# A fused attention and two-layer kernel: the value products of a turned head pair are placed behind the first run of scores, with a PSUM bank from another ring

## The chip, the cores and the metric

The kernel runs on one core of a Trainium2 chip. The metric is the device time of one execution in microseconds. Three runs of the kernel before gave 1013.64, 1014.48 and 1014.77 us; the median, 1014.48 us, is the number to be predicted for the changed kernel.

## What is computed

```python
scores = q @ k.T / 8                       # 8 batches x 8 heads, 576 x 576, head size 64
decay = cum[:, :, :, None] - cum[:, :, None, :]   # cum: running sum of log f
attn = softmax(where(causal, -1e9, scores + decay))
x = (attn @ v), heads side by side          # 4608 rows x 512
h = x @ w_in                                # 512 -> 2048
g = max(h, 0) + alpha * min(h, 0)
out = g @ w_out                             # 2048 -> 512
```

The matrix products are taken in parts (a high and a low half of each operand, three products for one), so that the result has more digits than one pass gives.

## The kernel before

**Work.** Heads go in 32 pairs (`n`, four pairs to a batch). Two heads of a pair share TensorE: each takes one half of it. Pairs 0 to 8 transpose their exponentials on TensorE; pairs 9 to 31 are *turned* (`turned`, L806): VectorE transposes blocks of 32x32 and sixteen DMAs put the blocks where they belong. When the four pairs of a batch are done, that batch of the first layer (`ffn1`: 16 groups of twelve 128x512 products, each group in one PSUM bank) can run. The second layer follows the attention.

**A turned pair on TensorE.** There are three pieces, all issued through `mm` (L364), so that the trace tells them by their tiles:

- *run 1* (L859 to L866, 24 matmuls, `bank<-Qhl`, 64 rows of the array by 128 columns): the scores of four query tiles, t3, t2, t0 and t1, of both heads. It takes six PSUM banks: `bA`, `bB`, `bC`, two each.
- *run 2* (L891 to L897, 6 matmuls, `bank<-Qhl`, the whole 128x128 array): the scores of the 64 tail queries of both heads. It writes one bank of its own, `bD`, and the free upper half of `bC[0]`, of which t1 of the first head fills the lower half.
- *the values* (`values` and `pv`, L933 to L953, 60 matmuls in the trace, `bank<-big,vr`, 128 rows by 64 columns): the exponentials of the pair **two before**, times v. The list `behind` holds the pairs whose values wait; `turned(n)` takes the oldest when there are two (L900). They write `bX` and 64 free columns of `bC[1]`, whose first 256 hold t1 of the second head. `done` then copies both with ScalarE (L958, L959).

The values need the sixteen moves of that pair (L919, half issued by SyncE, half by GpSimd, 100 KB each, `big<-big`), and its v (`vr`). This happens for n = 11 to 31, 21 times; the last two pairs' values have banks of their own at the end of pair 31 (L966).

**VectorE for a turned pair.** `shrink` (L846) adds the decay to a tile of scores and takes its minimum, reading PSUM: t3, t2, t0, then t1. `turn` (L879) transposes, in three parts; the tail's two reductions are L909. ScalarE takes the exponentials (L826).

**Order.** All operations are first listed with a cost, a due key, their dependencies and the ring that each buffer comes from. `Plan.run` (L116) then goes through time: on each engine it takes the operation that can start first, of equal starts the one with the lowest key. It does this before anything is issued; each engine's instructions then stand in that order. Costs are spread by a seeded random factor of up to 3% that is drawn as the operations are listed. The first layer has a key near 1e6 and so fills whatever TensorE has left; its evacuation has the key -1000 and goes first.

**Rings.** The eight PSUM banks are one store with rings on it: `rP` (turned pairs; at most 6), `rV` (values; at most 2; used by pair 8 alone), `rH` (first layer; 2 to 4), and others. A ring with `least` keeps that many banks from the others while it holds fewer; `rH.least` is 2 from the start and 0 once the last batch of the first layer is through. `swap_banks` (L1090) sets `rP.least` to 4 when the turned pairs begin.

```python
ns = 250 + c_row(512, 3) + c_row(384, 3) + c_row(128, 3) + c_row(256, 3)
s1 = s = op("PE", ns, run1, k0, rdy, bA + bB + bC + held)
...
bD, bX = Buf(rP), Buf(rP)
...
s = op("PE", ns, run2, k0 + 5, rdy, bC + [bD, bX] + held)
...
if len(behind) > 1:
    fn, vd, vb, done = behind.pop(0)(bX, bC[1])
    done(op("PE", ns_v, fn, k0 + 5.01, [s] + vd, [bX, bC[1]] + vb))
```

Of the kernel before, what the change touches and what calls it, by code (L numbers as in the profile page):

```python
# [94 lines left out]
class Plan:  # L95
# [7 lines left out]
    def op(self, eng, ns, fn, key, deps=(), bufs=(), two=False, kb=0.0):  # L103
        o = Op()
        ns *= self.rnd.uniform(0.97, 1.03)
        o.eng, o.ns, o.fn, o.key, o.bufs, o.two, o.kb = eng, ns / 1000.0 * SLACK.get(eng, 1.0), fn, key, bufs, two, kb
        o.outs, o.ready, o.end, o.n = [], 0.0, None, 0
        for b in bufs:
            b.left += 1
        for d in deps:  # L110
            if d is not None and d.end is None:
                d.outs.append(o)
                o.n += 1
            elif d is not None:
                o.ready = max(o.ready, d.end + self.lag(d, o))
        self.ops.append(o)  # L116
        return o
# [88 lines left out]
def attention_moe(  # L206
# [18 lines left out]
    op = plan.op  # L225
# [28 lines left out]
    rH, rO = Ring(banks, 2, 4), Ring(banks, 0, 6)  # L254
    rP, rV, rC = Ring(banks, 0, 6), Ring(banks, 0, 2), Ring(banks, 0, 1)
# [53 lines left out]
    def c_mm(n):  # L309
        return max(110, 13.3 + 0.4175 * n)  # L310

    def c_m4(n):
        return 5 + 1.67 * n

    def c_row(n, m):
        return m * max(110, 13.3 + 0.4175 * n)
# [226 lines left out]
    behind, later_x, quick_ops, value_ops, last_e = [], [], [], [], []  # L543
# [262 lines left out]
    def turned(n):  # L806

        b, p = divmod(n, NP)
        k0 = NS * n
        kl = k0 - 16  # L810
        held = []
        rdy, rz, rt, bZ, terms = load_n(n, held)
# [25 lines left out]
        def shrink(i, h, src, st, s, bank):  # L838
            w, col = 128 * (i + 1), (i if h == 0 else 5 + i)
            bE, e = block(i, h)  # L840

            def red():
                blk = lambda ap: ap.rearrange("p (j s) -> p j s", s=128)
                z = blk(bZ.t[0][:, h])
                in1 = (z[:, 6:7], z[:, 0:8:7], z[:, 0:9:4], z[:, 0:4])[i]
                ve.tensor_tensor_reduce(out=blk(e()), in0=blk(src()), in1=in1, scale=-0.125,  # L846
                                        scalar=3.0e38, op0=ALU.add, op1=ALU.min, accum_out=lo()[:, col : col + 1])

            r_ = op("DVE", c_dve(w) + 80, red, st, [s] + rz[h], [bank, bE, bst, bZ])
            expo(bE, e, w, col, st, [r_])  # L850
# [5 lines left out]
        bC = [Buf(rP), Buf(rP)]  # L856
# [7 lines left out]

        ns = 250 + c_row(512, 3) + c_row(384, 3) + c_row(128, 3) + c_row(256, 3)
        s1 = s = op("PE", ns, run1, k0, rdy, bA + bB + bC + held)  # L866
        for i, t, bank in ((3, t3, bA), (2, t2, bB), (0, t0, bB)):
            for h in range(2):
                shrink(i, h, lambda t=t, h=h: t(h), k0 + 0.1 * (4 - i), s, bank[h])
# [15 lines left out]
        turn(bE1, TA, CUT, k0 + 3, sums[3:], TA)  # L885
        seen = len(sums)

        bD, bX = Buf(rP), Buf(rP)
        part = ((0, 320, lambda: bD.t[:, 0:320]), (320, S, lambda: bC[0].t[:, 256:512]))

        def run2():  # L891
# [2 lines left out]
                    mm(out(), q()[:, 512:640], k()[:, c0:c1], c == 0, c == 2)  # L894

        ns = 100 + 6 * c_mm(288)
        s = op("PE", ns, run2, k0 + 5, rdy, bC + [bD, bX] + held)  # L897
        for h in (1, 0):
            shrink(1, h, lambda h=h: t1(h), k0 + 3.5, s1, bC[h])
        if len(behind) > 1:  # L900
            fn, vd, vb, done = behind.pop(0)(bX, bC[1])
            done(op("PE", ns_v, fn, k0 + 5.01, [s] + vd, [bX, bC[1]] + vb))

        e5 = lambda: bE2.t[:, 128 * (TAIL - CUT) : 128 * (TAIL - CUT) + S]

# [60 lines left out]
        while n == B * NP - 1 and behind:  # L966
            own = [Buf(rP) for _ in range(2)]
            fn, vd, vb, done = behind.pop(0)(*own)
# [34 lines left out]
    ns_v = 10 * c_m4(128) + 5 * c_m4(64) + 250  # L1003
# [80 lines left out]
    def swap(*what):  # L1084
        for st, ts in what:
            st.items += ts
            st.free += [(plan.t, i) for i in range(len(ts))]
        rT.least = 0

    def swap_banks():  # L1090
        swap((rE.store, [e_1]), (rE2.store, [e_2]))
        rS.least = 0
        rP.least = 4

    o_swap = op("-", 0, swap_banks, 0, last_e)
    op("-", 0, lambda: swap((rTa.store, [0, 1]), (rTb.store, [t_t])), 0, w_all + last_e)
    op("-", 0, lambda: swap((rM.store, m_t)), 0, [value_ops[-1]])
    op("POOL", 100, lambda: po.memset(e_0[:, 128 * TAIL + S :], 0.0), NS * NX - 22, [o_swap])
    for n in range(NX, B * NP):
        turned(n)  # L1100
# [298 lines left out]
```

## Time and profile before

| | us |
|---|---|
| runs | 1013.64, 1014.48, 1014.77 (median 1014.48) |
| span of the profiled execution | 1010.1 |
| TensorE busy in the span | 1004.1 (99%) |
| VectorE, ScalarE, GpSimd busy | 801.8, 614.0, 385.0 |

The profile's own execution is told by its span, first to last instruction; no time of its own stands beside it. The median of the runs is 4.4 us above that span. In the rows, PE is TensorE, DVE VectorE, ACT ScalarE, POOL GpSimd, SP SyncE; L364 is line 364 of the kernel. A timeline row gives start, length, engine, line, operation, output and input tiles, shape and the number of instructions merged in it. Matmuls are pipelined, so the ends of rows overlap the next row's start by some tenths of a us: the time that a block of matmuls takes is read from its start to the start of the next block.

### The profile page before, as it was taken

The page shows a single profiled execution, that of the slowest core. Times are in us where ns is not written, and L with a number is a line of the kernel's source. Part 1 is how long each engine was busy: PE and PEld are TensorE (multiplying, and loading weights), DVE is VectorE, ACT ScalarE, POOL GpSimd, SP SyncE. Part 2 cuts the span into 40 slices and gives each one's busy share as a digit, 9 for nine tenths or more (in the row PEclk, how much of TensorE's full clock was granted, in tenths as well). Part 3 has the DMA queues.
Part 4 walks back from the last instruction along what each step waited for, and adds up shares of the span by engine and source line. Part 5 has one row for each costly group of instructions (what it writes and reads, how often), then busy time and mean ns, then how long its engine had stood idle before and what let it go on. Part 6 is the DMA issues. An engine that isn't in the chain of part 4 may idle for free.

```text
span 1010.1 us, 22277 instructions
## 1 busy us (share of the span) xinstructions
PE 1004.1 (99%) x7928; PEld 894.0 (88%) x7928; DVE 801.8 (79%) x1745; ACT 614.0 (61%) x1379; POOL 385.0 (38%) x625
## 2 busy tenths in 40 slices
PE   9999999999999999999999999999999999999998
PEld 6788888888888888888888888999999999999998
DVE  6887778778778838777646888688898888989994
ACT  7888886666666646666444766564554645546551
POOL 4554658899898848877640100000000000000000
PEclk9999999999999999999999999999999999999999
DMA  6977856988888876878766665633434344434411
GB/s 206 263 228 235 263 142 187 279 260 253 255 242 248 239 219 202 243 222 254 209 194 231 210 231 185 209 111 120 152 123 143 111 144 131 140 112 139 136 53 43
DMA packets 130687, 191.14 MB, mean 189 GB/s; under 512 B 22088, under 2 KB 79728, under 8 KB 130576
## 3 DMA queue, kind: packets, MB, share of 16 engines
q1 hardware_dynamic: 124400, 170.66, 54.5%
q0 software_dynamic: 5888, 18.85, 6.9%
q8 instruction: 63, 1.03, 0.4%
q14 instruction: 48, 0.39, 0.1%
q10 hardware_dynamic: 288, 0.20, 0.1%
HBM read 102.74 MB, written 48.80 MB: 150 GB/s over the span
## 4 chain that ended last, share of the span: by engine, by line
PE 96%; DMA 2%; DVE 1%; issue 0%; DVEq 0%; ACT 0%; SPq 0%
PE bank L364 92%; PE bank L584 3%; DMA big<-big 1%; PE bank L466 1%; DVE big L879 1%; DMA hd<-hs 0%; PE bank L432 0%; DMA xt<-xs 0%; DVE hs L1036 0%; DVE big L846 0%; PE bank L651 0%; PE bank L725 0%; DVE hs L1327 0%; DVE big L429 0%; ACT hs L1034 0%
## 5 line engine op out<-in xcount | busy, mean ns | idle before, releaser
L364 PE MATMUL bank<-xx,wi 128*128 128x512 f32 x1728 | 412.3, 394 | 0.0
L364 PEld LDWEIGHTS bank<-xx,wi 128*128 128x128 f32 x1728 | 318.7, 188 | 69.0 <-DVE st L846 0.3
L826 ACT ACTIVATE big<-big,st 128x384 f32<-128x384 f32 (+4 forms) x207 | 119.2, 578 | 56.3 <-DVE st L846 53.0
L364 PE MATMUL bank<-wi,gh 128*128 128x256 f32 x1008 | 123.9, 283 | 0.0
L364 PE MATMUL bank<-wot,gh 128*128 128x256 f32 x1008 | 123.9, 283 | 0.0
L364 PEld LDWEIGHTS bank<-wot,gh 128*128 128x128 f32 x1008 | 122.3, 192 | 0.1
L364 PEld LDWEIGHTS bank<-wi,gh 128*128 128x128 f32 x1008 | 122.3, 192 | 0.0
L1034 ACT ACTIVATE hs<-bank,ab 128x512 f32<-128x512 f32 x96 | 65.6, 684 | 86.4 <-PE bank L364 58.0
L879 DVE STREAM_TRANSPOSE big<-big 128x1408 f32<-128x1408 f32 (+2 forms) x69 | 87.1, 1275 | 24.6 <-DMA hd<-hs 10.5
L1036 DVE SCALAR_TENSOR_TENSOR hs<-bank,sa,hs 128x512 f32<-128x512 f32 x96 | 70.3, 734 | 45.2 <-ACT hs L1034 44.5
L538 POOL TENSOR_TENSOR Qhl<-rqk,Qhl 128x640 fp32r<-128x640 f32 (+1 forms) x56 | 83.4, 1500 | 54.9 <-ACT Qhl L537 43.6
L919 POOL DMA_DIRECT2D big<-big x184 | 92.0, 507 | 14.7 <-issue 8.8
L364 PE MATMUL bank<-big,vr 128*64 128x128 f32 (+2 forms) x1884 | 95.5, 259 | 0.4 <-DVE st L609 0.2
L364 PEld LDWEIGHTS bank<-big,vr 128*64 128x64 f32 x1884 | 88.9, 137 | 7.6 <-DVE st L703 0.8
L364 PE MATMUL bank<-Qhl 64*128 64x512 f32 (+6 forms) x840 | 90.8, 323 | 0.7 <-DVE hs L1036 0.7
L364 PEld LDWEIGHTS bank<-Qhl 64*128 64x128 f32 (+1 forms) x840 | 76.6, 186 | 16.5 <-issue 6.3
L510 POOL TENSOR_TENSOR Z<-Z,tri 128x384 f32<-128x384 f32 x60 | 54.8, 923 | 32.8 <-DMA Z<-c 17.3
L846 DVE CUSTOM_DVE_ANT_1 big<-bank,Z 128x384 f32<-128x384 f32 (+1 forms) x92 | 41.8, 483 | 30.7 <-PE bank L364 30.3
L364 PE MATMUL bank<-wot,xx 128*128 128x256 f32 x504 | 62.4, 283 | 0.0
L364 PE MATMUL bank<-wi,xx 128*128 128x256 f32 x504 | 62.4, 283 | 0.0
L364 PEld LDWEIGHTS bank<-wi,xx 128*128 128x128 f32 x504 | 61.3, 192 | 0.0
L364 PEld LDWEIGHTS bank<-wot,xx 128*128 128x128 f32 x504 | 61.3, 192 | 0.0
(175 smaller groups left out, 1494.3 us busy)
## 6 DMA issues: line engine op xcount, KB each, us to landing
hd<-hs SPq DMA_DIRECT2D x144, 256.0 KB, 3.4
wx<-hd SPq DMA_DIRECT2D x46, 512.0 KB, 3.6
big<-big POOLq DMA_DIRECT2D x184, 100.0 KB, 4.9
big<-big SPq DMA_DIRECT2D x184, 100.0 KB, 4.8
rqk<-in_qk_dram SPq DMA_DIRECT2D x28, 608.0 KB, 5.1
hr<-hd SPq DMA_DIRECT2D x26, 512.0 KB, 3.5
vr<-in_vv_dram SPq DMA_DIRECT2D x32, 320.0 KB, 3.5
big<-in_w_in_dram SPq DMA_DIRECT2D x16, 512.0 KB, 5.4
```

What stands on the lines that cost most here:

```text
L364: pe.matmul(o, lhsT, rhs, start=start, stop=stop)
L466: pe.matmul(bank[:, 0:128], ident, ident, start=True, stop=True)
L510: m1 = op("POOL", c_po(128 * 3), lambda z4=z4: po.tensor_tensor(z4()[:, 6:9], z4()[:, 0:3], tb(3), ALU.add), kc + 0.1, got + [o_mask], [bZ])
L538: o2 = op("POOL", c_po(w), lambda hi=hi, lo=lo, raw=raw: po.tensor_tensor(lo(), raw(), hi().bitcast(F32), ALU.subtract), kc, [o1], [bqk, bQ])
L584: pe.transpose(t[:, c : c + 128], src[:, 128 * j : 128 * j + 128], ident)
L826: sums.append(op("ACT", c_exp(w), lambda: ac.activation(at(), at(), AF.Exp, bias=lo()[:, col : col + 1], scale=-1.0, accum_out=su()[:, col ...
L846: ve.tensor_tensor_reduce(out=blk(e()), in0=blk(src()), in1=in1, scale=-0.125, scalar=3.0e38, op0=ALU.add, op1=ALU.min, accum_out=lo()[:, ...
L879: ve.transpose(t_t[:, :, c0 : c0 + 32 * (b1 - b0)].rearrange("p k (b c) -> p k b c", c=32), bE.t[:, 128 * off : 128 * (off + b1 - b0)].rea ...
L919: moves.append(op(n_, 550 if i % 2 else 450, lambda a=a, k=k, q_=q_: q_.dma_start(bM.t[32 * k : 32 * k + 32, a], t_t[32 * a : 32 * a + 32, ...
L1034: cp = op("ACT", c_act(512), lambda bh=bh, bs=bs, fc=fc: ac.activation(bs.t, bh.t, AF.Relu, scale=ab[:, fc : fc + 1]), -1000, [last, o_sg] ...
L1036: cp = op("DVE", c_dve(512), lambda bh=bh, bs=bs, fc=fc: ve.scalar_tensor_tensor(bs.t, bh.t, sa[:, fc : fc + 1], bs.t, ALU.mult, ALU.add), ...
```

## The change

- The values of pair n - 2 are listed directly behind run 1 of pair n, with the key k0 + 0.01 in place of k0 + 5.01, and depend on run 1 (`s`) in place of run 2.
- Their bank `bX` comes from the ring `rV` and is taken when they start; before it came from `rP` and was taken when run 2 started.
- Run 2 takes one `rP` bank (`bD`) in place of two.
- When the turned pairs begin, `rH.least` falls from 2 to 1.

```diff
         s1 = s = op("PE", ns, run1, k0, rdy, bA + bB + bC + held)
+        if len(behind) > 1:
+            bX = Buf(rV)
+            fn, vd, vb, done = behind.pop(0)(bX, bC[1])
+            done(op("PE", ns_v, fn, k0 + 0.01, [s] + vd, [bX, bC[1]] + vb))
         for i, t, bank in ((3, t3, bA), (2, t2, bB), (0, t0, bB)):
...
-        bD, bX = Buf(rP), Buf(rP)
+        bD = Buf(rP)
...
-        s = op("PE", ns, run2, k0 + 5, rdy, bC + [bD, bX] + held)
+        s = op("PE", ns, run2, k0 + 5, rdy, bC + [bD] + held)
         for h in (1, 0):
             shrink(1, h, lambda h=h: t1(h), k0 + 3.5, s1, bC[h])
-        if len(behind) > 1:
-            fn, vd, vb, done = behind.pop(0)(bX, bC[1])
-            done(op("PE", ns_v, fn, k0 + 5.01, [s] + vd, [bX, bC[1]] + vb))
...
         rS.least = 0
-        rP.least = 4
+        rP.least, rH.least = 4, 1
```

## Rows read from the trace of the kernel before

**Rows 1.** The page: TensorE's busy time and granted clock in 40 slices.
```profile
PE 1004.1 (99%) x7928; PEld 894.0 (88%) x7928; DVE 801.8 (79%) x1745; ACT 614.0 (61%) x1379; POOL 385.0 (38%) x625
...
PEclk9999999999999999999999999999999999999999
```

**Rows 2.** TensorE's waits, 150 to 535 us: total, times, longest.
```profile
PE bank L364 <- DVE hs L1036: 0.7, 1, 0.7
PE bank L364 <- DVE big L879: 0.2, 1, 0.2
```

**Rows 3.** Timeline of TensorE, turned pair 15 and the start of pair 16.
```profile
232.79 2.19 PE L364 MATMUL bank<-Qhl 64*128 64x512 f32 x24
234.92 3.02 PE L364 MATMUL bank<-xx,wi 128*128 128x512 f32 x12
237.77 0.95 PE L364 MATMUL bank<-Qhl 128*128 128x320 f32 x6
238.66 2.98 PE L364 MATMUL bank<-big,vr 128*64 128x128 f32 x60
241.57 5.74 PE L364 MATMUL bank<-xx,wi 128*128 128x512 f32 x24
247.24 0.97 PE L364 MATMUL bank<-Qhl 64*128 64x512 f32 x6
```

**Rows 4.** Timeline of TensorE, pair 10, which has no values behind run 2.
```profile
161.69 0.96 PE L364 MATMUL bank<-Qhl 128*128 128x320 f32 x6
162.48 6.99 PE L364 MATMUL bank<-xx,wi 128*128 128x512 f32 x30
169.40 0.97 PE L364 MATMUL bank<-Qhl 64*128 64x512 f32 x6
```

**Rows 5.** Timeline of TensorE, pair 22.
```profile
336.64 2.19 PE L364 MATMUL bank<-Qhl 64*128 64x512 f32 x24
338.76 5.74 PE L364 MATMUL bank<-xx,wi 128*128 128x512 f32 x24
344.34 0.95 PE L364 MATMUL bank<-Qhl 128*128 128x320 f32 x6
```

**Rows 6.** Timeline of TensorE, pair 7: values right behind scores of 64 rows.
```profile
112.63 0.79 PE L364 MATMUL bank<-Qhl 64*128 64x384 f32 x6
113.35 2.98 PE L364 MATMUL bank<-big,vr 128*64 128x128 f32 x56
```

**Rows 7.** SyncE's moves of pair 14, and their times to landing (235 to 246 us).
```profile
237.33 6.66 SPq L919 DMA_DIRECT2D big<-big  x6
...
DMA to landing us min/median/max: 2.2/4.7/6.2
```

**Rows 8.** Timeline of TensorE: the block right behind run 1 of pair 16.
```profile
249.36 3.02 PE L364 MATMUL bank<-xx,wi 128*128 128x512 f32 x12
```

**Rows 9.** SyncE's moves of pair 11 with times to landing (190 to 199 us).
```profile
190.73 7.66 SPq L919 DMA_DIRECT2D big<-big  x8
...
DMA to landing us min/median/max: 4.7/5.9/7.2
```

**Rows 10.** Run 1 of pair 13 and what follows it on TensorE.
```profile
198.29 2.19 PE L364 MATMUL bank<-Qhl 64*128 64x512 f32 x24
200.42 3.93 PE L364 MATMUL bank<-xx,wi 128*128 128x512 f32 x16
```

**Rows 11.** SyncE's moves of pair 20 with times to landing (327 to 337 us).
```profile
330.27 6.22 SPq L919 DMA_DIRECT2D big<-big  x6
...
DMA to landing us min/median/max: 4.6/5.7/6.8
```

**Rows 12.** Timeline of VectorE in pair 15.
```profile
234.46 0.71 DVE L1036 SCALAR_TENSOR_TENSOR hs<-bank,sa,hs 128x512 f32<-128x512 f32 x1
235.09 0.67 DVE L846 CUSTOM_DVE_ANT_0 big<-bank,Z 128x512 f32<-128x512 f32 x1
...
237.69 0.08 DVE L846 DVE_READ_ACCUMULATOR2_ANT st<- 128x1 f32 x1
...
241.71 0.42 DVE L846 CUSTOM_DVE_ANT_1 big<-bank,Z 128x256 f32<-128x256 f32 x1 [0.71 <-PE bank L364]
```

**Rows 13.** The page: the first layer's evacuation on ScalarE.
```profile
L1034 ACT ACTIVATE hs<-bank,ab 128x512 f32<-128x512 f32 x96 | 65.6, 684 | 86.4 <-PE bank L364 58.0
```

## The prediction, as it was put on record

> **What bounds the kernel now.** I read the page first: TensorE is busy for 1004.1 of 1010.1 us, and its clock is at full grant (2.4 GHz) in all 40 slices [rows 1]. Its waits come next: between 150 and 535 us, where the turned pairs lie, there are two, 0.7 and 0.2 us [rows 2]. So no engine can give this stage anything by being quicker; the time is the sum of what TensorE issues. What can still shrink is the cost of an instruction in its place. That is read from the timeline of one pair, start of block to start of block [rows 3]: run 1 2.13 us, twelve first-layer matmuls 2.85, run 2 0.89, values 2.91, 24 first-layer matmuls 5.67. The same blocks elsewhere have other lengths, depending on their neighbours [rows 4, 5], and this is where the change works.
>
> The span is the time that I sum against. The median of the runs, 1014.48, is 4.4 us above it; I take that distance as unchanged.
>
> **The change part by part.**
>
> *The price of a neighbour.* Between run 1 and run 2, 12 first-layer matmuls take 2.85 us [rows 3] and 24 take 5.58 [rows 5]: 2.73 for 12, 0.2275 each. What is over is the cost of entering and leaving the block:
> - run 1, first layer, run 2: 2.85 - 2.73 = 0.12.
> - values, first layer, run 1: 5.67 - 24 x 0.2275 = 0.21 [rows 3].
> - run 2, first layer, run 1: 6.92 - 30 x 0.2275 = 0.10 [rows 4].
> - run 2 takes 0.89 ahead of values [rows 3] and 0.79 ahead of the first layer [rows 4]: 0.10 for run 2 to values, nothing for run 2 to the first layer.
>
> The pattern: going between the whole array (first layer, run 2) and its halves (run 1 by rows, values by columns) costs; staying on the whole array does not. From the second and third lines, entering the first layer behind values costs 0.21 - 0.10 = 0.11.
>
> *The sum for one pair.* Before: 0.12 + 0.10 + 0.21 = 0.43. After, with values right behind run 1, then first layer, run 2, first layer: 0.11 + 0 + 0.10 = 0.21. If run 2 should follow the values at once, the 0.11 is paid there instead, with the same sum. Gain 0.22 us.
>
> One joint is not in the turned pairs of this trace: run 1 to values. An earlier pair shows its like: six score matmuls of 64 rows by 384 columns take 0.72 us ahead of values [rows 6]. Per pair of heads that is 3 x 384 = 1152 columns; run 1 has 3840 in 2.13 us, so its share would be 0.64 with its entry and exit spread over all columns. At most 0.08 is left for a dearer exit. I take the exit as equal, because a short run must show its one entry and exit more than a long one; the ends are 0.14 us a pair (0.08 dearer) and 0.32 (no cost of leaving one split for the other, 0.10 less, as between run 2 and the first layer).
>
> *How many pairs.* The place exists 21 times, so the ceiling is 21 x 0.22 = 4.6 us. The values need the moves of the pair two before. In the steady case SyncE's last move of pair 14 is issued by 237.33 + 6.66 = 243.99 us and moves land 2.2 to 6.2 us after issue, median 4.7 [rows 7]; run 1 of pair 16 ends at 249.36 [rows 8]: some 1 to 3 us in hand. Pair 11's are issued until 198.39 with a landing of at least 4.7 [rows 9], while run 1 of pair 13 is over at 200.42 [rows 10]: some 2 us late. Pair 20's are issued until 336.49, the last about 1 us before that, and take 4.6 or more [rows 11], against 338.76 in pair 22 [rows 5]: about 1 late. Read so, of the 21 two are late, five have under 1.5 us, and the rest have more. The planner places the values when its own estimate of the landing is over, so a late pair gets first-layer work ahead of its values and keeps the old cost: no gain, no loss. I take 17 pairs: 17 x 0.22 = 3.7 us.
>
> *New waits.* Before, the values stood behind run 2, three to nine us further on, so a late move never showed. Now it does: TensorE is in order, and first-layer matmuls that could run are queued behind the values. If the estimate is early by up to 1 us in a few of the close pairs, that is about 1.0 us in all; the ends are nothing, and 8 us (first rival). I take 1.0, near the end without waits, because rows 2 show that the plan made no such error anywhere in this stage.
>
> *Banks.* Six for run 1 and one for the values leave one for the first layer, which is why its reserve falls to 1. In run 1 and values, 2.13 + 2.91 = 5.04 us, the first layer fills no new bank. Its last one is copied meanwhile: 0.68 us on ScalarE [rows 13] and 0.71 on VectorE [rows 12]. The first bank of run 1 is read by VectorE from 2.3 us after the start of run 1 [rows 3, 12]. So the first layer finds banks when the values are over. Run 2 asks for one bank in place of two, which can only bring it forward. I cost these at nothing; without the cover the price is a wait for one evacuation, about 1.4 us a pair.
>
> *VectorE and the bank that is shared.* VectorE waits 0.71 us for TensorE and reads t1 at 241.71, 0.14 behind the values' end at 241.57 [rows 3, 12]: t1 and the values share bC[1]. In the new place the values end 5.04 us after the start of run 1, and VectorE is done with t3, t2 and t0 at 237.77, 4.98 after it [rows 12]. So this wait goes away. It hid nothing that TensorE needs; I cost it at 0. The Trainium skill, page "PSUM — Partial Sum Buffer", section "PSUM bank collisions raise a hardware error", says that two engines may not touch one bank in the same 32 partitions at once even at different columns, so they must be kept apart by bank and not by address. The trace agrees: the read begins just when the writing ends. By that rule alone the change has a dark side, the third rival below.
>
> *Moved along:* the two copies by ScalarE and the quotient on GpSimd become ready some 4 us earlier; no DMA is added or taken away, and SyncE's queue is passed by none. Nobody waits for them in this stage. The draw of the random factors shifts within each pair, so the plan will differ in small ways everywhere behind 155 us; I put that into the range.
>
> *Sum:* 1010.1 - 3.7 + 1.0 = 1007.4 us of span, or 1014.48 - 2.7 = 1011.8 us.
>
> **The rivals.**
>
> 1. *Slower: the moves become TensorE's wait.* Mechanism: the values are written right behind run 1 in all pairs, and land-times run 1 us later against run 1 than in the rows of before. Price: the two late pairs wait about 3.5 and 2.3 us, five close ones about 0.5: 8 us against 4.6 of gain, so 3.5 us slower, 1018. It decides from a total wait of 4.6 us. For it: SyncE takes 6.7 us for six moves [rows 7], over 1 us each, where the planner reckons 0.45. Against: TensorE's waits are 0.9 us in 385 [rows 2], so the plan as a whole is not hasty.
> 2. *The change doesn't do what it says.* When run 1 ends, both other banks belong to the first layer, or the planner's own landing is later than the real one; first-layer work stays between. Then the joints are those of before, and the time 1013.7 to 1015. For: the bank that was filled right before pair 15's run 1 is free at 234.46 + 0.71 = 235.17 [rows 12], behind run 1's end at 234.92 [rows 3]. Against: one bank is enough, and the group before it had 2.7 us more.
> 3. *TensorE waits for VectorE's read of t1.* If a late pair's values are issued behind that read, they stand still until it is done; from the rows it would come some 7 us or more behind run 1's end [rows 3, 12] (against it: values so late are unlikely). Up to 2 us for one or two pairs; I count it within the first rival.
>
> **How the numbers follow.** About 0.2%, 2.03 us, is what a measurement of this kernel can tell from no change. My forecast has 0.55: 1010.0 to 1013.2, from 21 pairs at full gain without waits to 12 pairs with 1.5 us of waits; 0.45 of it lies below 1012.45, 0.10 above. No effect has 0.24, all within 0.2%. Slower has 0.21: 1015 to 1020, 0.17 of it beyond 1016.5 and 0.04 within. That makes 0.45 faster, 0.38 the same, 0.17 slower. The range takes in the forecast, no effect, and the near part of the slower case: 1010.0 to 1016.0. What is left out is chiefly the far part of rival 1.
>
> **What would show it.** In the timeline of TensorE, run 1 is followed by 60 matmuls of the values in most of 21 pairs, and run 2 by the first layer, at 0.79 us. Blocks of first-layer matmuls behind run 2 have 0.10 over, and those behind values ahead of run 2 have 0.11. VectorE's wait of 0.71 ahead of t1 is gone. TensorE's waits in the stage stay under 2 us. The prediction is wrong if its waits there exceed 4 us with a DMA or VectorE as releaser (rival 1 or 3), if first-layer matmuls stand between run 1 and values in most pairs (rival 2), or if run 1 takes over 2.2 us ahead of values, when the joint I took as equal is the error.

## The result, and the profile after

| | median us | runs | ratio to the kernel before |
|---|---|---|---|
| before | 1014.48 | 5 (1012.34 to 1015.01) | |
| changed | 1027.90 | 5 (1023.73 to 1030.32) | 1.0135 (1.0118 to 1.0151) |

The change makes the kernel 1.35% slower. The forecast was 1011.8 us, in a range of 1010.0 to 1016.0. The profiled execution of the changed kernel took 1027.9 us; its span is 1026.1, 16.0 more than the 1010.1 of the kernel before.

The page of the changed kernel, TensorE's busy time and clock:

```profile
span 1026.1 us, 22257 instructions
...
PE 1007.3 (98%) x7928; PEld 896.8 (87%) x7928; DVE 803.6 (78%) x1745; ACT 612.5 (60%) x1379; POOL 385.2 (38%) x625
...
PEclk9999999999999999999989999999999999999999
```

TensorE is busy 3.2 us longer than before and idle 12.8 us longer. So most of the loss is waiting, and not a longer sum of matmuls. The waits of TensorE, 150 to 560 us (total, times, longest), answer to [rows 2]:

```profile
PE bank L364 <- DMA vr<-in_vv_dram: 4.5, 2, 3.6
PE bank L364 <- DMA hd<-hs: 3.3, 1, 3.3
PE bank L364 <- DMA rd<-st: 2.9, 2, 1.6
PE bank L364 <- DVE hs L1037: 1.6, 2, 1.4
PE bank L364 <- DMA big<-big: 0.9, 1, 0.9
PE bank L364 <- DVE st L846: 0.3, 1, 0.3
```

Before, there were 0.9 us in two waits. Now 11.6 us in six waits end with a DMA, each a wait of values. Five of them, 7.9 us by the timeline, are at values that the change moves. The sixth, 3.6 us, is at the values of pair 30, which stand at the end of pair 31 in both kernels.

The DMA names must not be taken at their word: the values depend on their moves and their v alone, not on hidden values (`hd`) or reciprocals (`rd`). SyncE's transfers lie close together and the view names one that ended at that moment. Timeline of VectorE at two of these waits, to be held against TensorE's rows at 350.02 and 526.95 further down:

```profile
350.00 2.11 DVE L883 STREAM_TRANSPOSE big<-big 128x640 f32<-128x640 f32 x2 [3.84 <-DMA hd<-hs]
...
526.84 0.84 DVE L883 STREAM_TRANSPOSE big<-big 128x640 f32<-128x640 f32 x1 [4.44 <-DMA vr<-in_vv_dram]
```

This transpose of 640 columns (`turn`, L879 of the kernel before) writes where the moves of the pair before it read, so it needs the end of those moves, and it needs no v. In each of the six waits it starts at most 0.13 us ahead of the values. So it is the moves that both engines wait for.

The place is as forecast. Timeline of TensorE, pair 11, to be held against [rows 3]:

```profile
171.82 2.19 PE L364 MATMUL bank<-Qhl 64*128 64x512 f32 x24
173.94 2.98 PE L364 MATMUL bank<-big,vr 128*64 128x128 f32 x60
176.86 1.06 PE L364 MATMUL bank<-Qhl 128*128 128x320 f32 x6
177.76 6.99 PE L364 MATMUL bank<-xx,wi 128*128 128x512 f32 x30
```

Run 1 takes 2.12 us ahead of values (2.13 ahead of the first layer), values 2.92, run 2 0.90 behind values and ahead of the first layer, and the block of 30 behind run 2 6.92, as in [rows 4]. The joints cost 0.11 + 0.10 = 0.21 us, the sum that was forecast. Values stand right behind run 1 in 15 of 21 pairs; in the other six, six first-layer matmuls stand between. Four of the waits on moves are among the 15 (6.3 us), one among the six (1.6 us, pair 12).

And here is what eats it. A timeline of TensorE, pair 22, and SyncE's moves of pair 20, whose values these are, with the times to landing of the stretch 334 to 347 us; before: [rows 5, 11]:

```profile
344.57 2.19 PE L364 MATMUL bank<-Qhl 64*128 64x512 f32 x24
350.02 2.98 PE L364 MATMUL bank<-big,vr 128*64 128x128 f32 x60 [3.25 <-DMA hd<-hs]
```
```profile
336.62 9.16 SPq L920 DMA_DIRECT2D big<-big  x8
...
DMA to landing us min/median/max: 7.0/7.6/9.6
```

The issues last until 345.78, and the moves whose landing the view can tell took 7.0 to 9.6 us; run 1 is over at 346.7. TensorE stands for 3.25 us at values that cannot start, with first-layer matmuls queued behind them. In the kernel before the same values came 8.6 us behind the start of run 1 ([rows 5]: 0.89 behind 344.34), so a late landing could not show as a wait.

Some waits cost twice. Timeline of TensorE around 527 us, and the last moves of pair 30 on SyncE and GpSimd; then the same values in the kernel before:

```profile
526.95 5.60 PE L364 MATMUL bank<-big,vr 128*64 128x128 f32 x60 [3.60 <-DMA vr<-in_vv_dram]
532.48 13.92 PE L364 MATMUL bank<-xx,wi 128*128 128x512 f32 x60
```
```profile
517.33 0.51 SPq L920 DMA_DIRECT2D big<-big  x1
...
519.05 1.99 POOL L920 DMA_DIRECT2D big<-big  x4
```
```profile
512.25 2.98 PE L364 MATMUL bank<-big,vr 128*64 128x128 f32 x60 [0.18 <-DVE big L879]
```

Here GpSimd issues last: four of its eight moves leave only between 519.05 and 521.04, behind other work in its queue. Which move landed last no view tells. Behind the wait of 3.60 us the values run at the lower clock level, 1.2 GHz, for part of their time and take 5.53 us in place of 2.92.

The other place is run 1 of pair 19. Timelines of TensorE, VectorE and ScalarE:

```profile
300.02 0.97 PE L364 MATMUL bank<-Qhl 64*128 64x512 f32 x6
302.35 0.44 PE L364 MATMUL bank<-Qhl 64*128 64x384 f32 x1 [1.36 <-DVE hs L1037]
303.00 1.95 PE L364 MATMUL bank<-Qhl 64*128 64x384 f32 x17 [0.22 <-DVE hs L1037]
304.88 2.72 PE L364 MATMUL bank<-xx,wi 128*128 128x512 f32 x6
```
```profile
299.55 2.10 DVE L883 STREAM_TRANSPOSE big<-big 128x640 f32<-128x640 f32 x2 [4.63 <-DMA rd<-st]
301.58 1.37 DVE L1037 SCALAR_TENSOR_TENSOR hs<-bank,sa,hs 128x512 f32<-128x512 f32 x2
```
```profile
299.85 0.69 ACT L1035 ACTIVATE hs<-bank,ab 128x512 f32<-128x512 f32 x1 [5.71 <-DMA hd<-hs]
```

TensorE waits for a bank that VectorE's L1037 has to read, and L1037 stands in VectorE's queue behind the transpose, which has waited 4.63 us for moves. ScalarE's step of the same evacuation (L1035) has waited 5.71 us for a transfer of hidden values, which SyncE issued behind eight moves. So late moves reach TensorE by way of the first layer's evacuation too. Behind these 1.58 us of waits the rest of run 1 takes 1.2 us more than elsewhere (4.86 from 300.02 to 304.88, less 1.58, against 2.12), and the six first-layer matmuls 2.64 where the like in pair 21 take 1.59. The windows around the three places (busy times by engine, granted clock, DMA share, GB/s):

```profile
300.00:312.00 12.00, 10.41 (x100) 8.46 (x100) 7.73 (x20) 8.53 (x23) 9.54 (x14) 0.86 0.81 246
524.00:534.00 10.00, 7.05 (x67) 6.71 (x68) 3.56 (x7) 2.21 (x5) 5.75 (x10) 0.66 0.37 129
343.00:353.00 10.00, 6.75 (x93) 5.82 (x91) 5.96 (x11) 2.89 (x8) 5.28 (x8) 1.00 0.80 217
```

Behind the wait of 3.25 us at 350 the clock stayed full.

The account of the 16.0 us of span: waits in the view +12.6 (13.5 less 0.9), slower matmuls behind waits +4.8 (2.6 at pair 30's values, 1.2 and 1.05 at pair 19), a slower start +1.1 (the first twelve matmuls, L432, took 5.30 us and not 4.25, long ahead of the change), joints 15 x -0.22 = -3.3. That is 15.2. The rest, 0.8, is about what the view leaves out of the waits, since it counts from the modelled end of a matmul (the 3.25 at 350.02 is 3.33 by starts: 350.02 - 344.57 - 2.12). Of all this, the waits at values in their new place are 7.9 us; pair 30's values cost 6.2, and the way by the evacuation at pair 19 3.8.

### The profile page after: what moved, and what is told of

Same layout as the page of the kernel before. It is cut to its first block, busy times and chain, and to the rows that moved or that the text cites. A ratio compares the mean times of both kernels' runs of the same rounds, so it can differ in the third digit from the quotient of the medians.

```text
span 1026.1 us, 22257 instructions
## 1 busy us (share of the span) xinstructions
PE 1007.3 (98%) x7928; PEld 896.8 (87%) x7928; DVE 803.6 (78%) x1745; ACT 612.5 (60%) x1379; POOL 385.2 (38%) x625
## 4 chain that ended last, share of the span: by engine, by line
PE 85%; DMA 8%; DVE 3%; SPq 2%; ACT 1%; issue 0%; DVEq 0%
PE bank L364 81%; DMA big<-big 3%; PE bank L584 3%; DMA vr<-in_vv_dram 2%; DMA rd<-st 2%; SPq L920 1%; DVE big L883 1%; DMA rqk<-in_qk_dram 1%; PE bank L466 1%; DVE hs L1037 1%; DVE big L846 1%; PE bank L432 1%; ACT hs L1035 0%; DMA hd<-hs 0%; DVE Zt L493 0%
## 5 line engine op out<-in xcount | busy, mean ns | idle before, releaser
L364 PE MATMUL bank<-xx,wi 128*128 128x512 f32 x1728 | 408.0, 393 | 0.3 <-DVE st L846 0.3
L1037 DVE SCALAR_TENSOR_TENSOR hs<-bank,sa,hs 128x512 f32<-128x512 f32 x96 | 71.0, 742 | 72.5 <-ACT hs L1035 72.3
L1035 ACT ACTIVATE hs<-bank,ab 128x512 f32<-128x512 f32 x96 | 66.1, 688 | 84.0 <-PE bank L364 56.6
L364 PEld LDWEIGHTS bank<-big,vr 128*64 128x64 f32 x1884 | 91.6, 140 | 21.1 <-issue 15.1
L364 PE MATMUL bank<-big,vr 128*64 128x128 f32 (+2 forms) x1884 | 98.1, 263 | 11.9 <-DMA vr<-in_vv_dram 4.5
L364 PE MATMUL bank<-Qhl 64*128 64x512 f32 (+6 forms) x840 | 93.5, 327 | 1.6 <-DVE hs L1037 1.6
L1032 ACT ACTIVATE hs<-bank,sg 128x512 f32<-128x512 f32 x48 | 33.0, 688 | 34.9 <-PE bank L364 22.7
```

The lines of the kernel that those rows point to most:

```text
L364: pe.matmul(o, lhsT, rhs, start=start, stop=stop)
L1032: cp = op("ACT", c_act(512), lambda bh=bh, bs=bs, fc=fc: ac.activation(bs.t, bh.t, AF.Copy, scale=sg[:, fc : fc + 1]), -1000, [last, o_sg] ...
L1035: cp = op("ACT", c_act(512), lambda bh=bh, bs=bs, fc=fc: ac.activation(bs.t, bh.t, AF.Relu, scale=ab[:, fc : fc + 1]), -1000, [last, o_sg] ...
L1037: cp = op("DVE", c_dve(512), lambda bh=bh, bs=bs, fc=fc: ve.scalar_tensor_tensor(bs.t, bh.t, sa[:, fc : fc + 1], bs.t, ALU.mult, ALU.add), ...
```

## The experiments

I set out with three theories. **M**: the values stand at TensorE's head while their moves are on the way. **B**: one bank in reserve starves TensorE. **S**: the new draw of the planner's random costs is a bad one. Figures like "15 right behind run 1" or "in hand by the plan" in the expectations are of the planner's order and of the times that it reckons with; they are no times of the chip.

### More time between landing and values: 3 us, 1.5 us, -2 us

```diff
-            done(op("PE", ns_v, fn, k0 + 0.01, [s] + vd, [bX, bC[1]] + vb))
+            vo = op("PE", ns_v, fn, k0 + 0.01, [s], [bX, bC[1]] + vb)
+            vo.more = 3.0   # 1.5, -2.0
+            for d_ in vd:
+                d_.outs.append(vo)
+                vo.n += 1
+            done(vo)
...
-            return 0.6
+            return 0.6 + (b.more if a.eng in ("SP", "POOL") else 0.0)
```

> The changed kernel, but the planner reckons 3 us more from the landing of the moves and of v to the values; no instruction is added, only the order differs. Theory M (the values stand at TensorE's head while their last moves are still on the way, because the planner's landing is too early): the waits ahead of values, 12.8 us in the changed kernel, fall below 2 us, and the time is 1010 to 1015 us. Theory B (one bank in reserve for the first layer and the values' bank from another ring starve TensorE): the banks are as in the changed kernel, so it stays at 1023 to 1028. Theory S (the new draw of the random costs gives a bad plan, whatever is moved): another draw of luck, anything from 1014 to 1028.

> The kernel with 3 us more from landing to values once more, seed 66, one look at another execution: its waits ahead of values are on banks, not on moves. Theory M: no DMA as releaser of a wait over 0.5 us ahead of values; 1011 to 1017 us.

(The label of this one names seed 2; the kernel is that of the 3 us, seed 66.)

> The changed kernel (seed 66), but the planner reckons the values ready 1.5 us later: 6 values right behind run 1. Theory M: half of the way between the changed kernel and the one with 3 us; waits ahead of values 3 to 7 us, time 1014 to 1021 us. Theory S or B: anything from 1013 to 1028.

> The changed kernel (seed 66), but the planner reckons the values ready 2 us sooner after the landing of their moves: 18 values right behind run 1 in place of 15, and more of them with nothing in hand. Theory M: the dozen tight pairs wait up to 2 us longer each; waits ahead of values 25 to 40 us in place of 12.8, and the time is 1036 to 1055 us. Theory S or B: the order of the rest is close to that of the changed kernel, so 1020 to 1032, with no rule in the sign.

Measured: +3 us 1013.20 (ratio to before 1.0004, 0.9990 to 1.0018), and 1015.38 in a single further execution; +1.5 us 1018.55 (1.0042, 1.0023 to 1.0061); -2 us 1025.03 (1.0120, 1.0087 to 1.0154). TensorE's waits with +3 us, then with -2 us:

```profile
PE bank L364 <- DVE hs L1042: 4.4, 2, 2.5
```
```profile
PE bank L364 <- DMA vr<-in_vv_dram: 5.9, 2, 3.1
PE bank L364 <- DMA rd<-st: 3.0, 1, 3.0
PE bank L364 <- DMA hd<-hs: 2.7, 1, 2.7
PE bank L364 <- DVE hs L1042: 1.0, 1, 1.0
PE bank L364 <- DMA xt<-xs: 0.6, 1, 0.6
```

With 3 us no wait on a DMA is left, though this trace is of the longest of ten executions (1017.35 us), and by the median the whole loss is gone. What is left is a wait on a bank: L1042 is the first layer's second evacuation step, L1036 of the kernel before. But only 7 of 21 values still stand right behind run 1 there, so this run takes most of the change back too, and cannot by itself tell late moves from the place. The run with -2 us misses the expectation of theory M: 18 values stand right behind run 1, but the DMA waits add up to 12.2 us, not to 25 or more, and the time, which M put at 1036 to 1055, lies where S or B had it. They come as four waits of about 3 us and one of 0.6, five in all, one of the four again at pair 30's values; the other values wait for nothing that the view shows. My reading, which no run tests: a wait sets TensorE back against all transfers to come, so that most of the next values find their moves landed. What the run does show is that waits of this kind don't add up pair by pair, as I had priced them.

With 1.5 us the time lies between, but the trace does not carry the reason that was expected: 3.2 of its 4.5 us of waits are on banks (L1042, six times), 1.0 on a DMA.

### The banks without the place, and the reserve alone

The first run has the whole of this edit to the kernel before, the second its last line alone.

```diff
-        bD, bX = Buf(rP), Buf(rP)
+        bD = Buf(rP)
...
-        s = op("PE", ns, run2, k0 + 5, rdy, bC + [bD, bX] + held)
+        s = op("PE", ns, run2, k0 + 5, rdy, bC + [bD] + held)
...
         if len(behind) > 1:
+            bX = Buf(rV)
...
-        rP.least = 4
+        rP.least, rH.least = 4, 1
```

> The kernel before, with the values where they were (behind run 2), but with their bank taken from the other ring when they start, run 2 with one bank, and the first layer's reserve at 1: the change's banks without its place. Theory M: as the kernel before, 1013 to 1016 us, with no wait over 1 us ahead of values. Theory B: 1023 to 1028. Theory S: the operations are listed in the order of before with the same draws, so 1013 to 1018.

> The kernel before (seed 66) with the one change that the first layer's reserve falls from 2 to 1. Theory M: 1012 to 1016 us. Theory B: the reserve is what costs, 1018 to 1028.

Measured: banks 1018.04 (1.0044, 1.0028 to 1.0060), reserve alone 1015.96 (1.0026, 1.0013 to 1.0039). Waits of the first, 1.6 us at three of the values and 1.0 at run 1:

```profile
PE bank L364 <- DVE st L846: 1.6, 3, 0.7
PE bank L364 <- DVE hs L1037: 1.0, 1, 1.0
```

Both are above what M gave, below what B gave. A smaller reserve is not free: TensorE waits for VectorE to read a bank that is to be used again at once (L846 reads scores). The reserve alone has 3.3 us of such waits, 2.5 of them for the first layer's evacuation. The two kernels lose 3 to 5 us, and the changed kernel's own waits are chiefly on DMAs. The profiled execution of the first took 1014.00 us, the shortest of its ten, so the trace does not show where the rest of its median's loss lies. Each of these kernels is a new plan too, so that no share of this is proved to be the reserve's alone.

### Other draws: seeds 67 and 2

```diff
-SEED = 66
+SEED = 67   # 2
```

> The changed kernel with another seed for the planner's random costs (67 in place of 66). Theories M and B: the waits are of the place or of the banks and not of the draw, so 1021 to 1032 us. Theory S: as far from 1027.9 as seeds spread; if the seed was what made 1027.9, this one may give 1012 to 1020.

> The kernel before with seed 67: how far a draw alone moves it. Theories M and B: 1012 to 1018 us, TensorE's waits in the turned pairs under 4 us. Theory S: 1018 to 1030, the kernel before having been a lucky draw.

> The changed kernel with seed 2: 16 values right behind run 1, 10 of them planned with under 2 us in hand. Theory M: TensorE waits 6 to 15 us ahead of values and the kernel is 3 to 12 us slower than the kernel before with the same seed. Theory S: no slower than that kernel by more than 2 us.

> The kernel before with seed 2. All theories: 1013 to 1020 us, no DMA wait ahead of values over 1 us, since each value is planned with 5 us or more in hand. It is the pair to the changed kernel with seed 2.

| seed | before | changed |
|---|---|---|
| 66 | 1014.48 | 1027.90 |
| 67 | 1018.39 (1.0050, 1.0031 to 1.0069) | 1018.06 (1.0040, 1.0022 to 1.0057) |
| 2 | 1014.95 (1.0022, 1.0011 to 1.0034) | 1016.33 (1.0043, 1.0028 to 1.0058) |

(Ratios are to the kernel before with seed 66, on the same chip in the same session.) S is right in part: a draw alone moves the kernel before by up to 5 us, and the change costs 13.4, nothing, and 1.4. Both changed kernels miss what M gave: 1021 to 1032 with seed 67, and with seed 2 6 to 15 us of waits and a loss of 3 to 12. The kernel before lies just above M's 1018 with seed 67 and within its range with seed 2. Waits that end with a DMA are in each changed kernel's trace, 1.2 us with seed 67, 5.1 with seed 2, 11.6 with seed 66. They are in two of the kernels before as well, at the values of the last pair, which the change leaves in place: 0.9 us with seed 2, and with seed 67

```profile
PE bank L364 <- DMA hd<-hs: 1.6, 1, 1.6
```

Seed 2 loses clock too, behind its longest wait; these values take 4.5 us in place of 2.9, at a granted clock of 0.83 in the ten us around them:

```profile
219.89 4.58 PE L364 MATMUL bank<-big,vr 128*64 128x128 f32 x60 [2.87 <-DMA vr<-in_vv_dram]
```

### The same order, shorter moves

The decisive pair: nothing in the plan changes, and in the traces every engine has the same instructions in the same order. Each move carries 192 of 800 columns, and the values read those again and again; the attention's result is left out.

```diff
-                bM.t[32 * k : 32 * k + 32, a], t_t[32 * a : 32 * a + 32, k, 32 * TA * bTa.i : 32 * TA * bTa.i + CW]),
+                bM.t[32 * k : 32 * k + 32, a, 0:192], t_t[32 * a : 32 * a + 32, k, 32 * TA * bTa.i : 32 * TA * bTa.i + 192]),
...
-                                b0 = place(PLACE[t, h] + j)
+                                b0 = place(PLACE[t, h] + j) % 192
...
-                                b0 = place(TAIL + j)
+                                b0 = place(TAIL + j) % 192
```

> The changed kernel with seed 66 and the very same order on every engine, but each move carries 192 of its 800 columns (24 KB in place of 100); the values read those columns again and again, so the attention's result is left out. Only the moves get shorter. Theory M (TensorE waits for the last moves): the waits ahead of values, 12.8 us, fall below 4 us, and the time is 1010 to 1017 us. Theory B (bank reserve) or S (the order itself is bad, on VectorE, ScalarE or in the banks): the order is as before, so 1021 us or more.

> The kernel before (seed 66) with the same shortened moves: the control. Theory M: its values have 4.8 us or more in hand by the plan and no DMA wait, so shortening gives nothing there: 1010 to 1014.5 us. If it falls as much as the changed kernel does, the moves load something else (the DMA engines as a whole), and M is not shown.

Measured: changed 1008.34 (0.9955, 0.9938 to 0.9972), before 1013.47 (0.9998, 0.9987 to 1.0008). The changed kernel with short moves, its page, its move issues (KB, median us to landing) and its only wait, at pair 30's values:

```profile
PE 1002.8 (99%) x7928; PEld 894.1 (89%) x7928; DVE 803.8 (80%) x1745; ACT 613.6 (61%) x1379; POOL 384.7 (38%) x625
```
```profile
big<-big SPq DMA_DIRECT2D x184, 24.0 KB, 3.3
big<-big POOLq DMA_DIRECT2D x184, 24.0 KB, 3.4
```
```profile
PE bank L364 <- DMA vr<-in_vv_dram: 0.3, 1, 0.3
```

SyncE's moves land in 3.3 us in place of 5.5, and 19.6 us go (1027.90 - 1008.34); in the kernel before the same cut does nothing. So the changed kernel's loss comes from its moves, on which TensorE waits at the values and, by way of the evacuation, at run 1. It is neither the banks nor the order as such: both are unchanged here, and no bank wait is left. And with the moves out of the way the change is worth 1013.47 - 1008.34 = 5.1 us by the medians. The two profiled executions lie 3.5 us apart (1013.55 and 1010.05), and the joints give 3.3 of them; the other 1.6 of the medians no trace shows.

### Honest costs in the plan

SyncE's issue of a move is reckoned at 0.45 us by the planner; [rows 7] has 6 in 6.66, [rows 9] 8 in 7.66. So:

```diff
-            moves.append(op(n_, 550 if i % 2 else 450, lambda a=a, k=k, q_=q_: q_.dma_start(
+            moves.append(op(n_, 550 if i % 2 else 800, lambda a=a, k=k, q_=q_: q_.dma_start(
```

with 1.5 us more from landing to values (as above) for seeds 2 and 66; with 1000 in place of 800 and no margin, seed 2; and, for comparison, 3 us of margin alone, seed 2.

> The changed kernel, seed 2, where the planner reckons 0.8 us for a move's issue on SyncE (0.45 before) and 1.5 us more from landing to values; 11 values right behind run 1. Theory M: waits on moves ahead of values under 2 us, the joints give 2.4 us, so 1011 to 1014 us, below both kernels with seed 2 (1014.95 and 1016.33). If bank waits take the place of the waits on moves, 1015 to 1020.

> The same with seed 66: 7 values right behind run 1. Theory M: 1011 to 1015 us, waits on moves under 2 us. With bank waits in their place: 1015 to 1020, as with 1.5 us in hand alone (1018.55).

> The changed kernel, seed 2, with 1.0 us for a move's issue and no margin: 6 values right behind run 1, 12 with under 2 us in hand by this plan. Theory M: if the error of the plan is the issue alone, waits on moves under 2 us and 1013 to 1016 us; if it is the landing too, 4 us or more of them and 1016 to 1021.

> The changed kernel, seed 2, with 3 us in hand: 3 values right behind run 1. Theory M: no wait on moves over 0.5 us; the gain of the joints is gone as well (0.7 us), so 1013.5 to 1016 us, as the kernel before with seed 2 (1014.95).

Measured: 1010.77 (0.9975, 0.9964 to 0.9986), 1010.88 (0.9980, 0.9967 to 0.9992), 1012.46 (0.9994, 0.9982 to 1.0007) and 1015.45 (1.0013, 0.9997 to 1.0028). The first two lie just below the ranges that M gave, the third below both of its ranges, the fourth within its own. Waits of the first two, one line each:

```profile
PE bank L364 <- DVE hs L1042: 1.0, 1, 1.0
```
```profile
PE bank L364 <- POOL xx L994: 0.3, 1, 0.3
```

No wait on a move is left in any of the four. The first two beat both kernels: 0.25% and 0.20% below the kernel before, with 11 and 7 values right behind run 1. The third shows that the issue's cost alone, without a margin, takes the waits on moves away too (2.1 us of waits on banks remain). By joints, 11 pairs give 2.4 us and 7 give 1.5; measured are 3.0 and 2.9 (the kernel before had 1013.75 in that session), so a part is not the joints, and may be the luck of a plan. The kernel before was not run with 0.8 us for the issue; how much of these gains belongs to the change, and how much to a plan with better costs, is open.

## Why the prediction was wrong

- *Joints: right.* 0.21 us a pair was forecast for the new order and 0.21 read. Run 1 ahead of values costs no more than ahead of the first layer, the value taken between 0.14 and 0.32. In the kernel with short moves the change is a gain, as argued.
- *How many pairs: nearly right in number.* 17 were taken, 15 came. But the two pairs that the rows had as late were priced at nothing, since the planner was trusted to put first-layer work ahead of them. It did not: pairs 13 and 22 are among the 15 and wait 0.90 and 3.25 us. VectorE's wait ahead of t1 shrank from 0.71 to 0.20 us in pair 15, at no price.
- *New waits: the step that failed.* "If the estimate is early by up to 1 us in a few of the close pairs, that is about 1.0 us in all ... because rows 2 show that the plan made no such error anywhere in this stage." Measured, in place of 1.0: 7.9 us of DMA waits at the values that were moved. Another 6.2 us came at pair 30's values (3.6 of wait, 2.6 of lower clock), for which the prediction had no term, and 3.8 at run 1 of pair 19 by way of the evacuation. [rows 2] could not show an error of the landing: the moved values started 5.9 us or more behind the start of run 1 there, in place of 2.1, and that slack hid whatever the error was. The row that could show it I had quoted against the planner, in rival 1: over 1 us for an issue that is reckoned at 0.45. It had to decide.
- *Rival 1, at 0.21, was what happened in the main.* Moves became TensorE's wait. For the moved values, mechanism and place hold. It had 8 us of waits there and 7.9 came, but spread otherwise over the pairs, so that the equal sum is luck: the moves of pair 20 took 7.6 us to land in the median where [rows 11] have 5.7, and summing by pair is no good rule, as the run with -2 us shows. Its total, 3.5 us slower or 1018, was too low, because the stall at pair 30's unmoved values, the way by the evacuation and the lower clock were missing from it.
- *Rival 2* came true in six pairs; in one of them (pair 12) the values waited all the same.
- *Rival 3* is not seen: no wait of values ends with VectorE.
- *Banks at nothing: not quite.* In the changed kernel run 1 of pair 19 waits 1.6 us for an evacuation, near the 1.4 that was given for the case without cover. Alone, in the old order, kernels with them lost 3 to 5 us; in the changed kernel's order with short moves, no wait is on a bank.
- *The shuffle of the plan* was put into the range at about 1 us each way. It is worth up to 5 us between seeds of the kernel before. With seed 67 or 2 the change would have been within about 0.2% of no change; the loss of 13.4 us belongs to the change and this draw together.

## What to carry to other kernels

When an order is planned ahead, moving a consumer forward uses up the slack that hid the plan's errors: compare the plan's cost of each transfer with its rows (issue and landing) before counting on the move, and take "no waits so far" as proof only for the slack that there was. Correct the plan's costs first, then move: the same change lost 1.35% with an issue at 0.45 us and stood 0.2% below the kernel before at 0.8 with a margin, though with 7 of 21 values moved and not 15. And try a change under several draws before it is judged, since here a draw alone is worth 0.5%.

## What was not expected of the hardware

The landing of the same moves differs from order to order: the moves of pair 20 needed 5.7 us in the median in one order and 7.6 in the other. Over the whole run they took 5.5, and 3.3 when each carried a quarter of the bytes.

The length of a stall alone did not tell whether TensorE's clock fell. Behind one of 3.60 us matmuls ran at the lower level (0.66 of full in the ten us around it), behind one of 3.25 us in the same execution they did not. In the run with -2 us the values behind all four stalls of 2.69 to 3.11 us took 4.3 to 5.5 us in place of 2.9 (granted clock 0.66 to 0.83 of full in the ten us around each), and with +3 us those behind a bank wait of 2.54 us took 4.4 (0.83).
